# Weight conversion moved up by one unit, and the first group's gate moved from step 7 to the end of step 6, in a recurrence followed by a gated network

## The chip, the cores and the metric

The kernel runs on one core of a Trainium2 chip. The core has a matrix engine (PE, which multiplies, and PEld, its weight loads), a vector engine (DVE), a scalar engine (ACT), GpSimd (POOL), and a sync engine (SP) that here only issues DMAs. Each engine works through its own list of instructions in the order in which they were built, and waits at an instruction whose inputs are not ready. The metric is the device time of the whole program in microseconds, lower is better. Before the change it is 489.56 us, the median of three runs (487.96 to 491.08).

## The reference

```
state = zeros(B, H, D, D)                      # B, H, S, D = 4, 8, 768, 48
for t in range(S):
    state = alpha[:, :, t, :, None] * state + einsum('bhd,bhe->bhde', k[:, :, t], v[:, :, t])
    y[:, :, t] = einsum('bhd,bhde->bhe', q[:, :, t], state)
x = y.transpose(0, 2, 1, 3).reshape(3072, 384)
out = ((x @ w1) * (x @ w2)) @ w3 @ w_out       # w1, w2: 384x1024; w3: 1024x1024; w_out: 1024x384
```

q, k, v and alpha are float32. The four weights arrive as float64: on the chip they are 64-bit words whose two 32-bit halves the kernel turns into float32 by integer work.

## The kernel before, in words

**Part 1** is the recurrence, in N = 24 steps of 128 positions (six for each of the four batches). Step n of the loop holds work on several chunks: `scores(n)` (L344 on PE, masked by DVE in L347), `transposed(n+1)` (L304 on PE, copied by ACT in L306), `attend_state(n-1)` (L364) and `attend(n-1)` (L370, copied to the tile `x` by ACT in L374), `outer(n)` (L316, then L324 or L326 on DVE), `decayed(n+2)` (L282 on DVE: q and k times their decays), `logs(n+4)` (L251, later also L255 on ACT) and `decays(n+3)` (L266 or, from chunk 10 on, L269 on PE, then two exponentials L272 and L273 on ACT). Every second chunk sends three rows of its decays through DRAM (`ends`, `dec`, POOL) and scales the running state with them in `advance` (L333 to L335 on POOL).

**Conversion.** `load_gates` converts one unit of w1 and w2: 128 rows and 256 columns of each, 512 KB of raw words in two loads of 256 KB (L183). There are twelve units; the first six fill the half of the weights (`w12`, first half) that the gates of part 1's first four groups use. A unit is seven DVE instructions (L192, L195, L198, L199, L201, L211, L212) and three on ACT (L191, L196, L209). `fetch(k)` issues raw loads until k units are under way; `convert(k)` runs k pieces of the oldest unit, of four pieces each. There are three raw buffers (`rawp`).

**Gates.** Three chunks make a group of 384 positions. For group g the kernel stores the three `x` tiles to DRAM (`xd`; the stores wait in a list `later` and are issued on SP at the top of the next step by `store()`), loads them back as `xT` (`load_x`, L386), and splits them into three parts (`split_x`: L392 on ACT, L393 and L394 on DVE), because each float32 product is computed from rounded parts. A gate tile then multiplies x with w1 and with w2; each of the two halves is nine matmuls of 128x384 in three sets of three, one set for each part of x (L400), an ACT step (L409) and a DVE step (L411), and their product is stored by L475. `run(1)` takes one half of the list `fill`. `begin` says at which step a group is loaded; in the kernel before, group g is loaded at step 4+4g and split at step 6+4g, and steps take 0, 3, 3 and 2 halves in turn from step 6 on.

**Order of work.** The instructions are written in the order of the loop, but a scheduler that builds the program places them within each engine's list by its own estimates; what is said below of an order is the order in the built lists. `tc.issue_after(i)` keeps work from being placed ahead of instruction i; `ends_of_part1` holds the last L347 and the last L374.

**Part 2** continues with all gate tiles that are left (L425, L457, L461), converts and folds w3 with w_out (L502 to L515, the `folds`), and multiplies the stored gates with the folded weight (L530 to L532, then L400 with `w3o`).

## Time and profile before

| what | value |
|---|---|
| median of three runs | 489.56 us |
| profiled run, its span | 485.98 us, 484.2 us |
| PE busy, DVE busy, ACT busy, POOL busy | 455.1, 358.2, 276.2, 72.5 us |
| share of the chain that ended last: PE, DVE, DMA, ACT | 74%, 11%, 7%, 3% |
| bytes moved, mean rate | 80.29 MB, 166 GB/s |

How to read it: busy time is the time in which an engine works on an instruction, and the chain of work that ended last is followed back from the last instruction to what released each one. A timeline row gives start and duration in us, the engine, the line, the output and inputs and, where a merged row stands for more than one instruction, their count; in square brackets stands the idle time of the engine before it and what ended that. Rows with SPq are DMA issues, whose duration is the time the issuing takes and not the transfer. PEclk is the share of its full clock that PE was granted, DMA share the mean busy share of the sixteen DMA engines (overlapping packets let it pass 1).

### The profile page before, as it was taken

The page shows a single profiled execution, that of the slowest core. Times are in us where ns is not written, and L with a number is a line of the kernel's source. Part 1 is how long each engine was busy: PE and PEld are TensorE (multiplying, and loading weights), DVE is VectorE, ACT ScalarE, POOL GpSimd, SP SyncE. Part 2 cuts the span into 40 slices and gives each one's busy share as a digit, 9 for nine tenths or more (in the row PEclk, how much of TensorE's full clock was granted, in tenths as well). Part 3 has the DMA queues.
Part 4 walks back from the last instruction along what each step waited for, and adds up shares of the span by engine and source line. Part 5 has one row for each costly group of instructions (what it writes and reads, how often), then busy time and mean ns, then how long its engine had stood idle before and what let it go on. Part 6 is the DMA issues. An engine that isn't in the chain of part 4 may idle for free.

```text
span 484.2 us, 9992 instructions
## 1 busy us (share of the span) xinstructions
PE 455.1 (94%) x3824; PEld 431.0 (89%) x3824; DVE 358.2 (74%) x582; ACT 276.2 (57%) x550; POOL 72.5 (15%) x138
## 2 busy tenths in 40 slices
PE   3778779999998999999999998999999999999997
PEld 1567569899998989999989997999999999999996
DVE  2669899997989666999877896893466366677671
ACT  2666667776767545888665665755446333333330
POOL 2123132112202210212321111110111100000000
PEclk9989799999999999999999999999999999999999
DMA  9999999999899854547662353321219455556511
GB/s 171 189 194 215 241 190 201 242 189 236 180 231 215 208 166 133 182 158 230 216 232 75 98 195 95 134 83 50 81 56 268 146 153 172 173 178 179 179 50 49
DMA packets 155311, 80.29 MB, mean 166 GB/s; under 512 B 104672, under 2 KB 145760, under 8 KB 155264
## 3 DMA queue, kind: packets, MB, share of 16 engines
q1 hardware_dynamic: 149744, 65.23, 55.6%
q0 software_dynamic: 5520, 14.43, 9.1%
q8 instruction: 30, 0.49, 0.5%
q14 instruction: 17, 0.14, 0.1%
HBM read 57.58 MB, written 22.06 MB: 164 GB/s over the span
## 4 chain that ended last, share of the span: by engine, by line
PE 74%; DVE 11%; DMA 7%; ACT 3%; issue 2%; SPq 2%; POOL 0%; DVEq 0%; ACTq 0%; POOLq 0%
PE bank L400 60%; DMA raw<-in_moe_w_dram 5%; PE bank L344 4%; PE bank L370 3%; PE bank L364 2%; PE bank L304 2%; DVE x L394 1%; DVE x L393 1%; DMA dec<-ends 1%; PE bank L502 1%; DVE power L199 1%; PE bank L316 1%; PE bank L269 1%; DVE ms L347 1%; DVE mant L198 1%
## 5 line engine op out<-in xcount | busy, mean ns | idle before, releaser
L400 PE MATMUL bank<-x,w 128*128 128x384 f32 x1152 | 212.1, 338 | 1.7 <-ACT bank L425 1.2
L400 PEld LDWEIGHTS bank<-x,w 128*128 128x128 f32 x1152 | 199.9, 188 | 5.0 <-ACT bank L425 2.6
L400 PE MATMUL bank<-w3o,ab 128*128 128x384 f32 x576 | 100.2, 336 | 0.0
L400 PEld LDWEIGHTS bank<-w3o,ab 128*128 128x128 f32 x576 | 99.9, 188 | 0.0
L409 ACT ACTIVATE t<-bank 128x384 f32<-128x384 f32 x62 | 30.4, 493 | 63.9 <-PE bank L400 63.6
L425 ACT ACTIVATE bank<-bank 128x384 f32<-128x384 f32 x98 | 46.2, 475 | 32.0 <-PE bank L400 31.7
L475 POOL DMA_DIRECT2D abd<-ab x46 | 26.5, 575 | 135.6 <-DVE ab L461 127.5
L461 DVE TENSOR_TENSOR ab<-bank,r 128x384 f32<-128x384 f32 x45 | 24.8, 552 | 24.5 <-ACT bank L425 13.3
L531 DVE TENSOR_TENSOR ab<-abl,ab 128x1024 fp32r<-128x1024 f32 x24 | 29.4, 1224 | 13.6 <-ACT ab L530 13.6
L400 PE MATMUL bank<-wo,w3T 128*128 128x384 f32 x192 | 36.4, 336 | 1.9 <-DVE w3T L505 1.1
L530 ACT ACTIVATE ab<-abl 128x1024 fp32r<-128x1024 f32 x24 | 25.5, 1060 | 20.7 <-PE bank L400 18.8
L400 PEld LDWEIGHTS bank<-wo,w3T 128*128 128x128 f32 x192 | 33.4, 188 | 2.7 <-DVE w3T L505 1.4
L191 ACT ACTIVATE rest<-raw 128x512 f32<-128x512 uint32 (+1 forms) x36 | 23.3, 647 | 21.5 <-DMA raw<-in_moe_w_dram 20.6
L196 ACT ACTIVATE power<-power,rebias 128x512 uint32<-128x512 uint32 (+1 forms) x36 | 25.1, 699 | 18.3 <-DVE power L195 18.3
L344 PEld LDWEIGHTS bank<-qkT 48*128 48x128 f32 x384 | 25.4, 202 | 10.9 <-ACT qkT L306 4.1
L344 PE MATMUL bank<-qkT 48*128 48x128 f32 x384 | 30.3, 301 | 4.6 <-ACT qkT L306 3.0
L306 ACT COPY qkT<-bank 128x512 f32<-128x512 f32 x48 | 25.9, 587 | 15.2 <-PE bank L304 15.2
L411 DVE SCALAR_TENSOR_TENSOR o<-bank,t 128x384 f32<-128x384 f32 x24 | 13.4, 557 | 27.5 <-issue 15.3
L347 DVE TENSOR_TENSOR ms<-bank,keep 128x512 int32<-128x512 int32 x48 | 31.1, 682 | 2.2 <-PE bank L344 2.2
L282 DVE TENSOR_TENSOR qk<-kq,e 128x768 f32<-128x768 f32 x24 | 22.8, 951 | 9.0 <-ACT e L273 7.3
L532 DVE SCALAR_TENSOR_TENSOR ab<-ab,abl 128x1024 fp32r<-128x1024 f32 x24 | 29.2, 1218 | 0.0
L411 DVE SCALAR_TENSOR_TENSOR r<-bank,t 128x384 f32<-128x384 f32 x38 | 21.0, 552 | 10.9 <-PE bank L400 8.3
(75 smaller groups left out, 568.8 us busy)
## 6 DMA issues: line engine op xcount, KB each, us to landing
abl<-abd SPq DMA_DIRECT2D x24, 512.0 KB, 4.5
abd<-ab POOLq DMA_DIRECT2D x46, 192.0 KB, 2.9
raw<-in_moe_w_dram SPq DMA_DIRECT2D x16, 512.0 KB, 4.9
raw<-in_moe_w_dram SPq DMA_DIRECT2D x24, 256.0 KB, 4.8
xT<-xd POOLq DMA_DIRECT2D x9, 576.0 KB, 4.5
ac<-in_alpha_dram SPq DMA_DIRECT2D x24, 192.0 KB, 5.0
kq<-in_k_dram SPq DMA_DIRECT2D x24, 192.0 KB, 4.9
kq<-in_q_dram SPq DMA_DIRECT2D x24, 192.0 KB, 4.5
```

What stands on the lines that cost most here:

```text
L196: nc.scalar.activation(power, power, AF.Relu, scale=2.0 ** 23, bias=rebias)
L306: nc.scalar.copy(qkT[:, :, :, ds(DP * half, DP)], tp[half])
L344: nc.tensor.matmul(sc[i][:, j, :], qkT[r, 0, j, :], qkT[r, 1, j, :], start=True, stop=True)
L347: masked = nc.vector.tensor_tensor(ms[:, i].bitcast(I32), sc[i].bitcast(I32), keep_bc, op=ALU.bitwise_and)
L400: nc.tensor.matmul(p, w[part][i], x[part][i], start=start and part == parts[0] and i == 0, stop=stop and part == parts[-1] and i == n - 1, ...
L409: nc.scalar.activation(t, p1, AF.Copy, scale=(1.0 + 1.0 / P) * scale)
L411: nc.vector.scalar_tensor_tensor(to, p2, scale, t, op0=ALU.mult, op1=ALU.add)
L425: nc.scalar.activation(p, p, AF.Copy, scale=1.0 + 1.0 / P)
L475: (nc.gpsimd if late else nc.sync).dma_start(out=abd[g][:, f, :], in_=ab)
L530: nc.scalar.activation(t[:, 0], ab, AF.Copy, scale=1.0 - 2.0 ** -13)
L531: nc.vector.tensor_sub(t[:, 1], ab, t[:, 0].bitcast(FP32))
L532: nc.vector.scalar_tensor_tensor(t[:, 2], t[:, 0].bitcast(FP32), -1.0 - 1.0 / P, ab, op0=ALU.mult, op1=ALU.add)
```

## The change

The change has two aims. Raw words of three units are asked for in the preamble instead of one, so that DVE can convert a unit in each of the first steps; six units are then written to be done by step 5 instead of step 6. And the first group's gate starts earlier: its `x` tiles are stored by ACT's own DMA queue right after they are copied, instead of on SP at the top of the next step; its `xT` is loaded at step 3 on POOL's queue; and it is split at the end of step 6, with one half tile of its gate (nine matmuls) run there. All later groups begin one step earlier too, with the pattern of halves moved by one step. The numbers of halves are 38 in both kernels by the end of part 1.

```diff
@@ attend
         for half in range(2):
-            later.append((to[half, :, :, ds(c * C, C)], x[ds(DP * half, D)]))
+            move = to[half, :, :, ds(c * C, C)], x[ds(DP * half, D)]
+            if g:
+                later.append(move)
+            else:
+                nc.scalar.dma_start(out=move[0], in_=move[1])
@@ preamble
     decays(1)
-    convert(1, 1)
+    fetch(1)
     load_v(1)
+    fetch(2)
     load_kq(2)
     load_a(3)
+    fetch(3)
+    convert(1)
     decayed(1)
+    convert(2)
     load_v(2)
     load_kq(3)
     load_a(4)
@@ the loop
-    begin = {4 + 4 * g: (g, range(FH if g < 4 else KF)) for g in range(5)}
+    begin = {3 + 4 * g: (g, range(FH if g < 4 else KF)) for g in range(5)}
...
-        if n - 2 in begin:
-            g, tiles = begin[n - 2]
-            split_x(g, 0)
-            fill.extend(gate(g, f) for f in tiles)
-        pieces = (0, 3, 3, 2)[(n - 6) % 4] if n > 5 else 0
+        def split(n):
+            if n in begin:
+                g, tiles = begin[n]
+                split_x(g, 0)
+                fill.extend(gate(g, f) for f in tiles)
+
+        if n > 6:
+            split(n - 2)
+        pieces = (0, 3, 3, 2)[(n - 5) % 4] if n > 6 else 0
...
-        early = n < 7
+        early = n < 5
         if n < N - 2:
-            convert(1, 2 if n == 0 else 3)
+            convert(1)
...
         if n in begin:
-            load_x(begin[n][0])
-        convert(early and n > 2)
+            load_x(begin[n][0], nc.gpsimd if n == 3 else nc.sync)
+        convert(early)
         run(pieces > 1)
         decays(n + 3)
         if n < N - 2:
-            convert(early or n % 3 == 0)
+            convert(early or (n > 5 and n % 3 > 0))
+        if n == 6:
+            with tc.issue_after(ends_of_part1[0]), tc.issue_after(ends_of_part1[1]):
+                split(3)
+            run(1)
         run(pieces > 2)
```

In the built lists, `split_x` becomes L396, L397 and L398, the gate's matmuls L404, and the load of `xT` L390; lines above `attend` keep their numbers.

## The prediction

> **What bounds the kernel now.** I read the page first, then busy time by stage, then PE's timeline and waits, then DVE's and SP's timelines for the first 65 us, where the change works. The page's busy times, and its slices of PE and DMA:

> ```profile
> PE 455.1 (94%) x3824; PEld 431.0 (89%) x3824; DVE 358.2 (74%) x582; ACT 276.2 (57%) x550; POOL 72.5 (15%) x138
> ...
> PE   3778779999998999999999998999999999999997
> ...
> DMA  9999999999899854547662353321219455556511
> ```

> PE is busy 455.1 of 484.2 us and the change removes none of its matmuls. So only PE's idle time of 29.1 us can shrink or grow, and it lies in the first six slices (12.1 us each). Stage by stage (duration; busy us and count of PE, PEld, DVE, ACT, POOL; PEclk; DMA share; GB/s):

> ```profile
> 20.00:33.00 13.00, 10.02 (x172) 7.77 (x172) 8.43 (x15) 9.62 (x23) 4.04 (x9) 1.00 1.12 194
> 33.00:64.40 31.40, 25.85 (x376) 20.86 (x369) 29.07 (x51) 20.68 (x43) 6.69 (x12) 0.84 1.04 217
> 64.40:110.00 45.60, 44.17 (x526) 40.22 (x522) 44.18 (x79) 33.94 (x77) 11.42 (x18) 1.00 0.96 205
> ```

> From 33 to 64.4 us DVE is the fullest engine (29.07 of 31.40) and the DMA engines are full as well; from 64.4 on PE never rests long. PE's timeline at the border, which is where the gate's first matmuls start:

> ```profile
> 58.92 0.91 PE L266 MATMUL bank<-la,utri 128*128 128x384 f32 x2 [0.53 <-ACT la L251]
> 59.77 1.16 PE L344 MATMUL bank<-qkT 48*128 48x128 f32 x16
> 62.31 0.72 PE L304 MATMUL bank<-ident,qk 64*128 64x64 f32 x16 [1.38 <-DVE qk L282]
> ...
> 64.44 1.32 PE L400 MATMUL bank<-x,w 128*128 128x384 f32 x6
> 66.14 2.33 PE L400 MATMUL bank<-x,w 128*128 128x384 f32 x12 [0.38 <-DVE x L394]
> 69.47 0.44 PE L269 MATMUL bank<-la,sums 128*128 128x384 f32 x1 [1.01 <-ACT la L255]
> ```

> Step 7's own matmuls (L344, L304, L370, L316 at 59.77 to 64.44) run while DVE finishes the split. Nine gate matmuls are done at 66.14 + 3 x 0.19 = 66.7. After that PE's waits in the whole rest of the program are few (line waited for: total, times, longest):

> ```profile
> PE bank L344 <- DVE ms L347: 1.6, 2, 1.3
> PE bank L400 <- ACT bank L425: 1.2, 3, 0.8
> PE bank L400 <- DVE w3T L505: 1.1, 1, 1.1
> PE bank L269 <- ACT la L255: 1.0, 1, 1.0
> ```

> With 0.8 for L504 that is 5.7 us: the most that any reordering after 66.7 can save, beside the last drain. DVE before the border, its two idle times and the split:

> ```profile
> 27.02 0.96 DVE L282 TENSOR_TENSOR qk<-kq,e 128x768 f32<-128x768 f32 x1 [1.63 <-DMA kq<-in_q_dram]
> ...
> 32.78 0.36 DVE L326 TENSOR_TENSOR T<-bank,T 128x192 f32<-128x192 f32 x1 [2.33 <-POOL T L335]
> ...
> 63.37 1.35 DVE L393 TENSOR_TENSOR x<-xT,x 128x1152 fp32r<-128x1152 f32 x1
> ```

> And SP's issues, which are the supply:

> ```profile
> 53.64 1.50 SPq L386 DMA_DIRECT2D xT<-xd  x1
> 55.24 0.90 SPq L183 DMA_DIRECT2D raw<-in_moe_w_dram  x2
> ...
> 61.53 1.05 SPq L133 DMA_DIRECT2D kq<-in_q_dram  x1
> 62.68 1.91 SPq L183 DMA_DIRECT2D raw<-in_moe_w_dram  x2
> ```

> SP's row has no gap from 0.7 us on: one issue follows the other, and the long ones (2 to 3 us for a load that took 0.56 at the start) come although the buffers they fill had been free for 5 us or more. So DMA throughput, not buffers, sets SP's pace. The raw words of unit 7 are those issued at 55.24.

> [...] The trace has a DMA share of 1.04 to 1.12 through 20 to 64 us, which agrees that the engines are full; that a second queue helps nothing no run here shows yet. [...] after a wait of 2.18 us and thin work before it, PEclk is 0.53 between 50.7 and 58.0, and 16 L344 take 2.08 us there against 1.16.

> **The change part by part.**

> DVE. In the built list, L397 stands behind all the DVE work that stood ahead of L393, less step 7's two L347 (2 x 0.60 from start to start), plus all of unit 7 (2 x 0.33 + 5 x 0.60 = 3.66) and three instructions of unit 8 (L192, L195, L198: 1.26). Net +3.7 us. Between 17.4 and 63.4 DVE idles 7.7 us (1.37 + 1.63 + 2.33 + 0.70 + 0.94 + 0.69), of which the earlier raw words can fill most. Without any idle L397 would start at 63.4 + 3.7 - 7.7 = 59.4; with the 1.37 that no raw word fills, 60.8.

> DMA. Up to unit 8's raw words SP and the other queues carry what SP carried before up to unit 7's, plus 0.52 MB: at 217 GB/s 2.4 us. Unit 7's landed about 60.5 (second issue near 55.7, median 4.8 to landing), so unit 8's land near 62.9, and k and q of chunks 2 to 8 come 2.4 to 4.8 us later than before. DVE had margins there of 2.6 us (chunk 6: issued 38.40, 4.7 to landing, used 45.70) and 3.9 (chunk 8: landed 57.4, used 61.30), so it now waits a little for them in steps 3 to 6. Moving six stores and xT off SP's queue frees about 4.7 us of SP's issuing (0.9, 1.4, 0.9, 1.5)[...]. Between no help and 3 us of help (the share dips under 1 in places, 0.68 at 32.8 to 35.0), I take 1: 62.0.

> ACT. Its list has L191 of unit 8, then two L374, then L396, so L396 cannot start before unit 8's raw words. 62.0 + 0.57 + 0.52 + 1.16 = 64.3 for its end. Six more DMA issues at 0.33 to 0.93 (SP's rows for the same stores) are 2 to 5 us on ACT, spread over steps 1 to 3, where ACT has a third of its time free; behind them stand L196 and the exponentials, which DVE and POOL wait for. I count nothing on the path, up to 1.5 at worst. The load on POOL stands behind T's scaling for chunk 4 and ahead of the decays' rows that chunk 8 needs four steps later: nothing.

> PE. This is the costly part. In PE's list the nine L404 stand ahead of step 7's L344, L304, L370 and L316. Those ran before the split; now they wait for it. L397 and L398 end at 64.3 + 1.27 + 1.27 = 66.8, and the last three of the nine at 67.6, counting 0.25 each. PE will have idled from about 59 to 64, so it is cold: step 7's four groups, 3.3 us warm (1.10 + 0.50 + 1.02 + 0.62), take 4.3 if a third of them runs at half clock. PE reaches the same state that it had at 66.7 at 67.6 + 4.3 = 71.9, which is 5.2 later. Off that goes PE's wait for L255 (1.0), which now falls into the time PE waits anyway. Sum +4.2; everything behind is PE's fixed work.

> Free edits: later groups loaded and split a step earlier move 9 to 18 matmuls among steps that are full; 38 halves stay 38. The loads of part 1 end near 165 us in both, since their bytes are the same.

> **The rivals.**

> Break-even: DMA has the slack, L397 starts at 60.8. Then 60.8 + 2.5 + 0.6 + 3.3 = 67.2, +0.5 less 1.0: 489, or 487 if some later waits go too. For it: DVE's bubbles at 27 and 32 us are the very places that earlier raw words fill, and the second queue may run where SP's stalls. Against: SP without a gap.

> Faster: break-even at the border with 0.5 us gained, and nearly all (5 us) of the 5.7 us of later waits goes, because one unit's conversion is out of the way and groups are split a step earlier: 489.6 - 0.5 - 5 = 484. Against: several of these waits have nothing to do with the border (L425, L505 and L504, 3.1 us together, lie at 240 to 300 us).

> Much slower: ACT's issues stall like SP's (1.5), raw words land at 62.9 and PE is cold for all of step 7: +8, 497.5.

> **How the numbers follow.** The stalled split 48% (489.6 + 4.2 = 493.8, about half of it on each side of +4.9 us, which is 1%), much slower 15%, break-even 28%, faster 9%. So slower by over 1%: 0.24 + 0.15 + 0.01 = 0.40; faster by over 1%: 0.09; within: 0.51. The range reaches from within break-even, 488, to past the much slower case, 499; what is left out is the faster case and the lower end of break-even, and a little above.

> **What would show it.** Right: a PE wait of 3 to 6 us ahead of the first L404, ended by L396 or L397; unit 8's L191 released by DMA just before; PEclk near 0.5 in the following 3 us; L344 of step 7 starting near 67 instead of 59.8. Wrong: L397 starting before 62, or DVE without waits for q and k in steps 2 to 5. The prediction fails outright if raw words land early because two queues move more than one, or if the PE stages after 70 us open or close gaps of several us that this trace has no sign of.

## The result, and the profile after

The changed kernel takes 518.84 us (median of four runs, 517.22 to 520.8) against 489.64 us in the same session: ratio 1.0599, 95% interval 1.0548 to 1.065. It is slower by 29 us, where 4 were predicted and 499 us was the upper end of the range. Here and below, medians are of all runs, while ratios and intervals leave out slow ones (over 1.5% above the fastest of the same kernel).

The page of the changed kernel: busy time, then the slices of PE, of PE's granted clock and of the DMA engines.

```profile
PE 472.9 (92%) x3824; PEld 443.4 (86%) x3824; DVE 361.9 (70%) x582; ACT 278.2 (54%) x550; POOL 73.0 (14%) x139
...
PE   3688399799899898999999899899999999999997
...
PEclk9988869969889799799999999999999999999999
DMA  9999998969969632255756335332115835555611
```

The span is 516.5 us against 484.2. PE runs the same 3824 matmuls but is busy 17.8 us longer, and its idle time has grown from 29.1 to 43.6 us (516.5 - 472.9), by 14.5. The longer busy time is the odd part: the same matmuls took longer. PEclk tells why. The clock record behind it shows half clock (0.50) in seven separate stretches, the last from 206.9 to 213.8 us and 51.2 us in all, where the kernel before had 10.2 us and was at full clock from 57.7 us to the end.

The first gate, in PE's timeline of the changed kernel:

```profile
58.71 0.91 PE L266 MATMUL bank<-la,utri 128*128 128x384 f32 x2 [2.07 <-ACT la L251]
64.88 4.05 PE L404 MATMUL bank<-x,w 128*128 128x384 f32 x9 [5.25 <-ACT x L396]
68.86 2.08 PE L344 MATMUL bank<-qkT 48*128 48x128 f32 x16
...
74.18 3.39 PE L404 MATMUL bank<-x,w 128*128 128x384 f32 x18
```

and in ACT's:

```profile
62.42 0.68 ACT L191 ACTIVATE rest<-raw 128x512 f32<-128x512 uint32 x1 [0.76 <-DMA raw<-in_moe_w_dram]
63.11 0.65 ACT L374 COPY x<-bank 128x256 f32<-128x256 f32 x2
63.65 1.18 ACT L396 ACTIVATE x<-xT 128x1152 fp32r<-128x1152 f32 x1
```

This is the stall that was predicted. Unit 8's raw words release L191 at 62.4, L396 follows, PE has waited 5.25 us for it, and step 7's L344, at 59.77 before, starts at 68.86. The state that PE had at 66.7 before (nine gate matmuls and step 7's own work done) it now has at 74.18, 7.4 us later.

But PE's waits in the whole trace (line waited for: total us, times, longest) show that this is not all:

```profile
PE bank L404 <- ACT x L396: 9.9, 5, 5.3
...
PE bank L404 <- ACT bank L429: 4.1, 5, 1.9
PE bank L404 <- DVE x L397: 3.3, 4, 1.5
...
PE bank L404 <- DVE x L398: 1.7, 3, 0.6
```

PE waits for L396 five times, not once. The other four are the borders between groups, at 100, 136, 171 and 205 us. The first of them, on PE and on ACT:

```profile
94.69 3.44 PE L404 MATMUL bank<-x,w 128*128 128x384 f32 x18
97.97 0.52 PE L269 MATMUL bank<-la,sums 128*128 128x384 f32 x2
99.82 0.79 PE L404 MATMUL bank<-x,w 128*128 128x384 f32 x3 [1.34 <-ACT x L396]
102.14 2.66 PE L404 MATMUL bank<-x,w 128*128 128x384 f32 x6 [1.52 <-DVE x L397]
```

```profile
97.87 0.85 ACT L413 ACTIVATE t<-bank 128x384 f32<-128x384 f32 x2
98.61 1.16 ACT L396 ACTIVATE x<-xT 128x1152 fp32r<-128x1152 f32 x1
```

The 18 matmuls at 94.69 are the last two halves of group 0. Only when they have ended (98.1) does L396 write group 1's first part, PE takes three matmuls, waits for L397, and goes on. xT had been issued at 76.84. The same border in the kernel before, on PE and on ACT and DVE:

```profile
84.16 3.39 PE L400 MATMUL bank<-x,w 128*128 128x384 f32 x18
...
95.72 3.44 PE L400 MATMUL bank<-x,w 128*128 128x384 f32 x18
```

```profile
91.08 1.18 ACT L392 ACTIVATE x<-xT 128x1152 fp32r<-128x1152 f32 x1
...
93.25 1.34 DVE L393 TENSOR_TENSOR x<-xT,x 128x1152 fp32r<-128x1152 f32 x1
94.52 1.35 DVE L394 SCALAR_TENSOR_TENSOR x<-x,xT 128x1152 fp32r<-128x1152 f32 x1
```

Group 0's last matmuls end at 87.55 there and group 1's first start at 95.72. The whole split lies between them, while PE works on the recurrence. Stretches around three of the borders (us; PE busy and count; PEclk; DMA share; GB/s), changed kernel:

```profile
95.00:112.00 17.00, 14.10 (x99) 0.70 0.93 208
131.00:147.00 16.00, 13.66 (x115) 0.79 0.78 160
166.00:181.00 15.00, 12.95 (x101) 0.77 0.67 167
```

and the same stretches of the kernel before:

```profile
95.00:112.00 17.00, 17.00 (x193) 1.00 0.95 202
131.00:147.00 16.00, 16.00 (x197) 1.00 1.05 238
166.00:181.00 15.00, 14.65 (x218) 1.00 0.55 176
```

PE idles 2 to 3 us at each border, and then runs at half clock for 7 to 10 us, so that it gets through about half as many matmuls (99, 115 and 101 against 193, 197 and 218). From the 10th gate matmul to the 343rd, which is the first of part 2, the changed kernel needs 149.2 us (74.18 to 223.42) and the kernel before 127.4 (66.74 to 194.12): 21.9 us more, 5.5 for each of four borders. With 7.4 at the first gate and 3.0 later, in part 2, that is the whole difference of the two profiled spans (32.3; the medians differ by 29.2).

### The profile page after: what moved, and what is told of

It reads as the page before. It is cut to its first block, busy times and chain, and to the rows that moved or that the text cites. A ratio compares the mean times of both kernels' runs of the same rounds, so it can differ in the third digit from the quotient of the medians.

```text
span 516.5 us, 9994 instructions
## 1 busy us (share of the span) xinstructions
PE 472.9 (92%) x3824; PEld 443.4 (86%) x3824; DVE 361.9 (70%) x582; ACT 278.2 (54%) x550; POOL 73.0 (14%) x139
## 4 chain that ended last, share of the span: by engine, by line
PE 44%; DVE 7%; DMA 5%; ACT 2%; issue 2%; ACTq 0%; DVEq 0%
PE bank L404 42%; DMA raw<-in_moe_w_dram 4%; DVE ab L465 1%; DVE x L398 1%; DVE power L199 1%; PE bank L506 1%; DMA raw<-in_moe_w_out_dram 1%; DVE x L397 1%; PE bank L370 1%; DVE mant L198 1%; DVE w L201 1%; ACT x L396 0%; DVE mant L192 0%; DVE wo L488 0%; PE bank L344 0%
## 5 line engine op out<-in xcount | busy, mean ns | idle before, releaser
L404 PE MATMUL bank<-x,w 128*128 128x384 f32 x1152 | 219.7, 344 | 19.1 <-ACT x L396 9.9
L404 PEld LDWEIGHTS bank<-x,w 128*128 128x128 f32 x1152 | 202.2, 191 | 27.9 <-ACT x L396 11.8
L404 PE MATMUL bank<-w3o,ab 128*128 128x384 f32 x576 | 100.2, 336 | 0.0
L404 PEld LDWEIGHTS bank<-w3o,ab 128*128 128x128 f32 x576 | 99.9, 188 | 0.0
L429 ACT ACTIVATE bank<-bank 128x384 f32<-128x384 f32 x98 | 46.4, 476 | 32.3 <-PE bank L404 31.7
L535 DVE TENSOR_TENSOR ab<-abl,ab 128x1024 fp32r<-128x1024 f32 x24 | 29.4, 1225 | 13.8 <-ACT ab L534 13.8
L344 PEld LDWEIGHTS bank<-qkT 48*128 48x128 f32 x384 | 29.4, 228 | 10.1 <-ACT qkT L306 4.9
L404 PE MATMUL bank<-wo,w3T 128*128 128x384 f32 x192 | 36.2, 335 | 1.9 <-DVE w3T L509 1.1
L344 PE MATMUL bank<-qkT 48*128 48x128 f32 x384 | 34.9, 331 | 3.4 <-ACT qkT L306 3.3
L191 ACT ACTIVATE rest<-raw 128x512 f32<-128x512 uint32 (+1 forms) x36 | 23.4, 649 | 26.5 <-DMA raw<-in_moe_w_dram 23.0
L347 DVE TENSOR_TENSOR ms<-bank,keep 128x512 int32<-128x512 int32 x48 | 31.3, 684 | 8.9 <-PE bank L344 8.9
L404 PEld LDWEIGHTS bank<-wo,w3T 128*128 128x128 f32 x192 | 33.4, 188 | 2.5 <-DVE w3T L509 1.4
L196 ACT ACTIVATE power<-power,rebias 128x512 uint32<-128x512 uint32 (+1 forms) x36 | 25.0, 697 | 14.8 <-DVE power L195 12.9
L370 PE MATMUL bank<-ms,v 128*64 128x128 f32 x384 | 31.9, 319 | 0.0
```

The costliest lines, as they stand in the source:

```text
L344: nc.tensor.matmul(sc[i][:, j, :], qkT[r, 0, j, :], qkT[r, 1, j, :], start=True, stop=True)
L347: masked = nc.vector.tensor_tensor(ms[:, i].bitcast(I32), sc[i].bitcast(I32), keep_bc, op=ALU.bitwise_and)
L370: nc.tensor.matmul(to, vc[:, 2 * j + i, :], ms[:, i, j, :], start=(n % NCH == 0 and j % HP == 0), stop=(j % HP == HP - 1), skip_group_chec ...
L404: nc.tensor.matmul(p, w[part][i], x[part][i], start=start and part == parts[0] and i == 0, stop=stop and part == parts[-1] and i == n - 1, ...
L429: nc.scalar.activation(p, p, AF.Copy, scale=1.0 + 1.0 / P)
L535: nc.vector.tensor_sub(t[:, 1], ab, t[:, 0].bitcast(FP32))
```

## The experiments

Theory A: `x3`, the split x, has one buffer (`tr0`, `bufs` 1), so the split of group g+1 has to wait for the last matmul that reads group g's. In the kernel before, a group's eight halves end in the three steps 3, 3, 2, and the split lies in the step with none: a whole step hides it. In the changed kernel the group has taken one half in step 6, three in step 7 and two in step 8 when the next split comes, in step 9: six of eight. Two halves spill into step 10, and there the last read, the split and the first use stand in a row. Theory B: the conversions moved up and the new order of the DMAs cost the time all through part 1. A third, C, came up for the buffer itself: the split is late because of its place in ACT's list or because xT is late.

**Only the first group moved.** In the code, `(...)` stands for what stays.

```diff
-    begin = {3 + 4 * g: (...) for g in range(5)}
+    begin = {4 + 4 * g - (g == 0): (...) for g in range(5)}
-        if n > 6:
+        if n > 7:
             split(n - 2)
-        pieces = (0, 3, 3, 2)[(n - 5) % 4] if n > 6 else 0
+        pieces = (0, 3, 3, 2)[(n - 6) % 4] - (n == 9) if n > 6 else 0
```

> The changed kernel with only the first group moved: its half tile stays at the end of step 6, later groups are loaded and split at steps 8, 12, 16, 20 and 10, 14, 18, 22 as in the kernel before, and all eight halves of a group end before the next group is split. Theory A (the split of group g+1 has to wait until the last matmul of group g has read the single x3 buffer, and two halves of every group now spill past the split; about 5.5 us at each of four group borders, beside 7.4 us at the first gate): 496 to 499 us, with no PE wait for L396 after the first gate. Theory B (the earlier conversions and the DMA order cost the time all through part 1): 510 us or more.

Measured: 495.26 us against 487.44 (ratio 1.0153, 1.0091 to 1.0214). PE waits for L396 once, 4.5 us, at the first gate. So the later groups' part of the loss is gone. B falls: conversions, stores and loads are all still there. What is left, 7.8 us, is not all the first gate:

```profile
64.44 3.95 PE L404 MATMUL bank<-x,w 128*128 128x384 f32 x9 [4.54 <-ACT x L396]
...
71.38 3.39 PE L404 MATMUL bank<-x,w 128*128 128x384 f32 x18
...
99.53 1.11 PE L304 MATMUL bank<-ident,qk 64*128 64x64 f32 x16 [1.34 <-DVE qk L282]
```

The state that PE had at 66.7 before, it has at 71.38 here, 4.6 us later (7.4 in the changed kernel). By the 82nd gate matmul (105.53 against 97.41) it is 8.1 us behind: it waited for L282 at 99.5 and ran at half clock from 98.9 to 105.7. This second loss seems to come from the test itself, which takes one half out of step 9. The kernel further below that keeps both halves there shows no such wait.

**The spill alone, in the kernel before.**

```diff
-        pieces = (0, 3, 3, 2)[(n - 6) % 4] if n > 5 else 0
+        pieces = (0, 3, 3, 2)[(n - 6) % 4] - 2 * (n == 7) if n > 5 else 0
```

> The kernel before with one edit: step 7 takes one half tile instead of three, so that two halves of each group are still to do when the next group is split, as in the changed kernel; nothing else of the change. Theory A: four stalls of PE at the group borders ended by L392 to L394, half clock after each, 511 to 514 us. Theory B: 489 to 492 us.

Measured: 503.91 us (ratio 1.0312, 1.0236 to 1.0387). The direction is A's, 15 us, but the size is below what A said. Part 1 holds 36 halves here, two fewer than before. A second set of runs of the same kernel gave the trace that is read below.

> The same kernel as the one with the spill alone, which came out at 503.9 us where 511 to 514 were expected; taken again for a second profile. Theory A: four stalls ended by L392, L393 and L394, together 8 to 9 us of PE idle time, and the rest of the loss as half clock after them, so that the loss differs with how many half-clock windows they set off: 501 to 511 us. If the spill costs no more than its idle time: 496 to 498.

Measured: 504.58 us against 487.61 (1.0353, 1.0296 to 1.0411). PE's waits in this trace:

```profile
PE bank L400 <- ACT x L392: 4.0, 4, 1.3
...
PE bank L400 <- DVE x L393: 2.4, 4, 0.6
PE bank L400 <- DVE x L394: 2.3, 4, 0.9
```

Less 0.4 for L394 at the first gate, the four borders idle 8.3 us. The kernel loses 17.0. PE is busy 467.4 us here against 455.1, 12.3 more, with the same matmuls; up to 260 us it runs 34 us at half clock against 10. Of these 34, 17 lie at two of the four borders (from 101.0 and 169.3 us) and 7 at 66.9 us, ahead of the first. Estimated from these numbers, the borders cost 8.3 us of waits and half of 17 us, about 17 us. In the changed kernel all four borders set off half clock, 31 us in all: that is why 15 to 17 us came out where 22 were expected.

**One half spilled instead of two.** In the same line, `- (n == 7)` instead of `- 2 * (n == 7)`.

> The kernel before with step 7 taking two halves instead of three, so that one half of each group spills past the split of the next group instead of two. Theory A (the split waits for the last reader of x3, however many are left): the last half and the first half of the next group now stand back to back with nothing between them, so the same four stalls, each a little longer (by the 0.5 us of two L269): 502 to 512 us. If the cost grows with the number of matmuls that spill: half of the other's, 495 to 497.

Measured: 503.33 us (1.0333, 1.0286 to 1.0379). Half the spill costs as much: what counts is that the last reader of the buffer comes after the split's place, not how much comes after it. The loss is made up differently in its trace: the borders' waits are longer, as expected (9.6 us), and half clock follows only two of them, 7 us in all.

**The changed kernel with three halves in step 6**, so that no half spills.

```diff
                 split(3)
-            run(1)
+            run(3)
```

> The changed kernel with three half tiles in step 6 instead of one, so that a group's eight halves are done before the next group is split; everything else of the change stays. Theory A: only the first gate's stall is left, 495 to 499 us, and no wait for L396 after 70 us. Theory B: 515 us or more, as the changed kernel.

Measured: 493.08 us against 487.44 (1.0106, 1.0075 to 1.0136). A change of one digit brings back all of the borders' loss. PE waits for L396 once (4.4 us). It came out 2 us under the expectation. Part 1 holds 40 halves here instead of 38, so the two kernels also differ by two halves moved from part 2 to part 1.

**A second buffer.** A second whole x3 would take 13.8 KB more per partition. Instead, x3 was cut into its three parts and part 0 alone given two buffers. The constant `after` moved into a tile that is written later, to make room; halves spill as in the change. The main line of the edit:

```diff
-        t = tr[i].tile([C, 3, KM, TG], FP32R, tag="x3", name="x3")
+        t = [tr[i].tile([C, KM, TG], FP32R, tag=f"x3{p}", name=f"x3{p}", bufs=2 - (i > 0 or p > 0)) for p in range(3)]
```

> The changed kernel with x3 as three tiles, one for each part, and a second buffer for part 0 alone (to make room, the constant that is needed once lies in a tile that is written later, and its rounded copy serves as the weights of the first decays). Halves still spill past the split. Theory A (the split waits for the buffer): L396 of groups 1 to 4 runs several us ahead of its first use, part 1 is written while part 2 of the last half is read, and the stalls at the four group borders shrink from about 5.5 us to 1.5 or less; the first gate's stall stays: 496 to 502 us. Theory C (the split is late because of the place that L396 has in ACT's list or because xT comes late, not because of the buffer): 515 us or more.

Measured: 498.22 us against 487.03 (1.0238, 1.0185 to 1.0291). L396 of group 1 in this kernel's ACT timeline:

```profile
82.52 1.15 ACT L396 ACTIVATE x<-xT 128x1152 fp32r<-128x1152 f32 x1
```

It runs 16 us earlier than in the changed kernel; the next three run at 116.74, 144.05 and 170.24 instead of 134.53, 169.44 and 203.37. PE's waits are 0.6 to 1.0 us in all at each of the last three borders, under the 1.5 that A allowed. At the first border PE still waits 2.4 us, now for L397, and half clock follows (99 to 109 us), so this border got no cheaper. Whether L397 is late there for its place in DVE's list or for its own single buffer is not shown. C falls for the other three: the same list of halves, the same loads, and the stall goes with the buffer. The total is some 4 us above the kernel with only the first group moved (1.0153).

**The split at the end of step 6, without the half tile there.** As the kernel with only the first group moved, but `run(1)` taken out and step 9 left at two halves.

> As the kernel with only the first group moved, but without the half tile in step 6: the split stays at the end of step 6, and the first L404 stands behind step 7's L344, L304, L370 and L316 again, as in the kernel before; conversions, stores and loads as in the change. Theory A: no stall at any group border and none ahead of step 7: 488 to 492 us; the first gate's stall then came from the nine matmuls' place in PE's list. If the late raw words cost by themselves wherever the matmuls stand: 493 to 496. Theory B: 510 or more.

Measured: 490.48 us against 487.44 (1.0077, 1.0056 to 1.0097). With step 7's own matmuls back in front of the first gate matmul, the state that PE had at 66.7 before comes at 67.74, and 3.6 of the 4.6 us that the kernel with only the first group moved loses there are gone. So the greater part of that stall comes from the nine matmuls' place in PE's list, as predicted. No wait for L282 comes near 99 us either. The 3 us that remain of the median are what the conversions, the queues and the earlier split cost together. Two of these alone cost 4.6 and 2.9 us (below), so the parts do not simply add up.

**The preamble and the pace of conversions alone**, in the kernel before (the change's edits to `fetch`, `convert` and `early`, and no others).

> The kernel before with only the change's conversions: raw words of three units in the preamble, and its pace of conversions; gates, stores, loads and splits as before. Theory A: q and k come up to 3 us later, which DVE's margin covers in part: 488 to 491 us (ratio to before 1.00 to 1.008). If filling DVE's idle time at 25 to 33 us were worth something by itself: 484 to 486.

Measured: 491.66 us against 487.03 (1.0101, 1.0071 to 1.0132), just above what was expected. On ACT and PE:

```profile
47.77 0.70 ACT L191 ACTIVATE rest<-raw 128x512 f32<-128x512 uint32 x1 [1.27 <-DMA raw<-in_moe_w_dram]
```

```profile
52.73 1.65 PE L266 MATMUL bank<-la,after 128*128 128x384 f32 x2 [3.13 <-ACT la L251]
```

ACT waits at L191 for raw words, and the logarithm behind it in its list (L251), which PE needs, comes late. DVE's idle time at 25 to 33 us was filled, but PE did not come forward by it: its L266 at 43.82 before starts at 44.18 here, and the one at 50.70 at 52.73. The DMA engines were full before (share 1.12 from 20 to 33 us) and are so here (1.12); the q issues of chunks 3 to 9 end 0.4 to 3.7 us later. That other loads came later for the earlier raw words fits this and is not shown by a run of its own.

**The queues alone**, in the kernel before (the first group's stores on ACT's queue, its load on POOL's at step 3).

> The kernel before with only the change's queues: the first group's x stored by ACT's queue, its xT loaded by POOL's at step 3; split and gates at their old places. Theory A: [...] SP gains a few us of issuing, ACT loses a few: within 1.5 us of before. If a second queue moves more: q, k and raw words land 2 us or more earlier, 485 or less.

Measured: 489.96 us against 487.03 (1.0072, 1.0043 to 1.0101), outside the 1.5 us. Unit 7's raw words are issued 1.1 us earlier (up to 55.06 instead of 56.14), with xT out of SP's way; q of chunk 8 at 53.60 against 53.49. From 20 to 60 us the DMA engines moved 224 GB/s against 212. That is no clear gain: the kernel with one half spilled, which leaves the queues as they were and is written like the kernel before up to step 7, moved 222 GB/s there and issued unit 7's raw words 1.3 us earlier. So neither that a second queue helps nor that it cannot is shown. The loss is on ACT:

```profile
50.83 1.16 ACT L396 ACTIVATE x<-xT 128x1152 fp32r<-128x1152 f32 x1 [3.60 <-DMA xT<-xd]
```

With the load at step 3, the scheduler has put the split's first part so early in ACT's list that ACT waits for the transfer, and PE behind it 3.8 us for the next logarithm (52.46; 2.2 before). DVE waits 3.0 us for L196, which also stands behind L396, and the L282 for which PE waited 1.4 us at 62.3 before now keeps it waiting 3.9 us, until 66.06.

None of these versions beats the kernel before.

## Why the prediction was wrong, point by point

**What bounds the kernel.** Half right. PE stayed the bound and its idle time grew by 14.5 us, but the larger part of the loss, 17.8 us, is busy time at half clock. The sentence "only PE's idle time of 29.1 us can shrink or grow" left this out; the sum has it for step 7 alone.

**DVE, DMA, ACT at the first gate.** Right, and close. Unit 8's raw words were put at 62.0 and released L191 at 62.4; L396's end was put at 64.3 and came at 64.8; PE's wait at 3 to 6 us and was 5.25. The q issues of chunks 3 to 9 end 1.4 to 4.6 us later than before, and DVE waits 0.6 us for one of them, at 53.35. ACT's six issues took 3.5 us of its time (five of 0.31 to 0.46 and one of 1.56), within the 2 to 5 that were taken. The 1 us of help from the freed issuing on SP was the author's estimate.

**PE at the first gate.** The mechanism was right, and the size depends on where the half clock ends. In the changed kernel's trace the nine matmuls took 4.05 us, and step 7's four groups 5.3 (68.86 to 74.18) where 4.3 was taken: nearly all of them, not a third, ran at half clock. So 7.4 us instead of 5.2. The refund for L255 came: no such wait is left. In the traces of the kernel with only the first group moved and of the one with the second buffer, the same matmuls in the same order come 4.6 and 4.7 us late: half clock ended there at 68.1 and 68.4, before step 7's groups. So 5.2 lies between what these traces show, and that is partly luck.

**"Free edits: later groups loaded and split a step earlier move 9 to 18 matmuls among steps that are full; 38 halves stay 38."** This is the step that failed, and it carries 22 of the 32 us between the two profiled spans. The count was right and was the wrong thing to count. What had to be asked was which halves are still to do when the next group is split: six of eight done instead of eight. What it put at nothing is four stalls of about 5.5 us, each a wait for the single buffer of x3 and, in the changed kernel, half clock after it. Both signs could be read before the run: in PE's built list the last 18 matmuls of group 0 stand beside the first nine of group 1 with only two L269 between, and the pool of x3 (`tr0`) has one buffer. The prediction had named the right symptom as its outright failure, gaps after 70 us that the trace of before has no sign of, but had no cause for it. A wait for a buffer does not show in the trace of before, because the step without halves hides it there.

**The rivals.** Break-even and faster are excluded. The much slower case, +8, had the first gate with PE at half clock for all of step 7, and that part came to 7.4 us in the changed kernel's trace; no rival had a stall that comes back with each group.

**What stays open.** Of the three microseconds lost in part 2, PE's waits for L429 are the visible part (4.1 us against 1.2 for L425 before). They differ from version to version (1.8 to 5.5). Which order of conversions there makes them was not tried. That half clock, and not only the idle time, makes the size of a border is read from busy times and PEclk; a version that keeps PE at full clock across the borders was not run. Each version but the spill alone was profiled once, so differences of one or two microseconds between single traces may be chance.

## What to carry to other kernels

When a stage of a pipeline is moved against another, a count of work per cycle is not enough: for each single buffer that the stage writes, look up where its last reader now stands, and whether there is still work of others between that reader and the first use of the new content. A wait in an engine's list also holds up what stands behind it (in the kernel with the queues alone ACT stood 3.60 us at L396, and PE waited 3.8 us, 2.2 before, for the logarithm behind it), so put the first use of a late result behind the work that does not need it, as the kernel before did with step 7's matmuls. And an idle engine is not worth filling for its own sake: here, with the DMA engines full (share 1.12 from 20 to 33 us), asking for its data earlier cost 4.6 us.
